# Group 1 of a convolution and MLP kernel: the run outermost on its partitions, one transfer each for x, y and output, and two first products moved ahead of a copy of w1

## The chip, the cores and the metric

The kernel runs on one core of a Trainium2 chip. The time is device time in microseconds of one execution. The engines are TensorE (PE, its weight loads PEld), VectorE (DVE), ScalarE (ACT), GpSimd (POOL) and SyncE (SP, which only issues DMAs here). DMAs are issued from SP's, ACT's or POOL's queue and are carried out by the core's 16 DMA engines.

## The reference

x has shape (8, 4224, 192), float32. First a causal depthwise convolution along the sequence with 7 taps; the taps are shared by the 24 channels of each of 8 heads and are a softmax over the 7. Then a residual block: normalise, multiply by a gain, up to 768 channels, ReLU, down to 192, add.

```python
w = exp(weight - max(weight)); w = w / (sum(w) + 1e-9)        # (8 heads, 7 taps)
y[b, s, h, :] = sum_k w[h, k] * x_pad[b, s + k, h, :]         # 6 zero rows ahead of x
yn = (y - mean(y)) / sqrt(var(y) + 1e-6) * g_ln
out = y + relu(yn @ w_ch1) @ w_ch2                            # 192 -> 768 -> 192
```

## The kernel before

**Groups.** The rows of x are cut into 17 groups (`groups`). A partition holds a run of neighbouring rows, with the 6 rows ahead of it, which the taps need. Of each batch the first 4096 rows lie as 128 runs of 32 rows; the 128 rows left of each of the 8 batches make up one group of their own, group 1 (`b is None`): 8 batches x 16 runs x 8 rows, one run to a partition. In the kernel before, partition 16 b + p holds run p of batch b, so each batch is a block of 16 neighbouring partitions, and each transfer of the group is made batch by batch: `load_x` (L141 to L148) issues batches 0 to 3 from SP and 4 to 7 from POOL, `store_y` (L487) issues eight stores from SP, `add_to_out` (L949) eight accumulating stores from POOL; the last two take their pieces from `rows_of_out`. All arithmetic is by partition and doesn't ask which row lies where.

**Stages of a group.** `first_tap` writes y = tap 0 times x on ACT (L378, one instruction for each head); `conv` adds the other taps on VectorE (L415); in some groups `second_tap` makes a product on ACT that a DMA adds. `transpose` turns y into 32 x 32 blocks on VectorE (L426). `up` multiplies by w1 on TensorE (L531) and `evict_up` writes the ReLU of it out of PSUM on ACT (L521). `down` multiplies by w2 (L796). The result, times the inverse deviation, is added to y, which has already been stored to the output, by an accumulating DMA (`add_to_out`). From group 2 on the products are made from quarters with fewer multiplications (L859).

**The order.** The kernel writes its order out by hand; each engine's instructions run in the order in which they are recorded, and semaphores hold one that needs another's result. A queue's DMAs are issued in order too.

**The start, where most of the change lies.** The weights come as 64-bit words and are put together by VectorE and ACT (`split_words`, `join_...`). `centre_w1` then makes the centred w1: three heads of group 0's convolution run on TensorE (`conv_on_pe`, L326, evicted at L330), and `copies_of_w1` copies rows of w1 to all four blocks of 32 partitions by matmuls (L352, L355), which ACT evicts into `w1` (L360): first chunks 0 to 3 of the left half, then chunks 4 and 5 of both halves, then `up(0)` begins. In `up(0)`, set f of 6 uses four PSUM banks, taken in turn from eight (`take_set`), and its matmuls go through the six chunks of w1 in order:

```python
banks = take_set()
rows_of_tiles(banks, yt[g][:, 0:n], w1[:, :, f * P : f * P + P])
evict_up(g, f, banks[:, :, 0 : n * C])
if g == 0 and f == 0:
    first_tap(1, heads=(0, H // 2))
elif g == 0 and f == 1:
    copies_of_w1(1, [(q, 1) for q in range(NQ)])
    scale_power(words_2[2])
elif g == 0 and f < 4:
    first_tap(1, heads=(2 * f, 2 * f + 2))
```

So ACT meets group 1's first four products between the evictions of set 0 and set 1. `copies_of_w1(1)` takes the four banks of set 0, so set 2 takes those of set 1 and waits for that eviction. `load_x(1)` is issued after the load of w2 (`raw`, L988), behind a small write of VectorE that holds it back (`gate`, L139).

Of the kernel before, what the change touches and what calls it, by code (L numbers as in the profile page):

```python
# [11 lines left out]
ALU = mybir.AluOpType  # L12
# [4 lines left out]
def kernel(  # L17
# [29 lines left out]
    nc = tc.nc  # L47
    PSUM = bass.MemoryType.PSUM
    B, S, D = x.shape
    H, K = weight.shape  # L50
    F = moe_w_ch1.shape[1]
    P = 128
# [3 lines left out]
    PAD = K - 1  # L56
    J = 16
    R = 2 * J
    LEFT = (S - P * R) * B // P
    LP = P // B  # L60
# [33 lines left out]
    def rows_of_out(g, j1, j2):  # L94

        b, j0, n = groups[g]
        if b is not None:
            return [(slice(0, P), outr[b, :, (j0 + j1) * D : (j0 + j2) * D])]
        left = out[:, P * R : S].rearrange("b (p r) d -> b p (r d)", p=LP)
        return [  # L100
            (slice(LP * b, LP * b + LP), left[b, :, j1 * D : j2 * D]) for b in range(B)
        ]

    consts = ctx.enter_context(tc.tile_pool(name="consts", bufs=1))
    xpool = ctx.enter_context(tc.tile_pool(name="xin", bufs=2))
# [14 lines left out]
    def take_bank():  # L120
        i = turn[0] % 8
        turn[0] = i + 1
        return all_banks[:, i]

    def take_set():
        i = (turn[0] + 3) // 4 * 4 % 8
        turn[0] = i + 4
        return all_banks[:, i : i + 4]
# [4 lines left out]
    def load_x(g, queue=nc.sync, pad=True, gate=False):  # L133
        b, j0, n = groups[g]
        t = xpool.tile([P, J + PAD, D], F32, tag="xg", name=f"xg{g}")
        xg[g] = t
        flat = t.rearrange("p j d -> p (j d)")
        if gate:
            nc.vector.memset(t[0 : 1 if b is not None else P, 0:1, 0:1], 0.0)  # L139
        if b is None:  # L140
            for b in range(B):  # L141
                (queue if b < B // 2 else nc.gpsimd).dma_start(  # L142
                    out=flat[LP * b : LP * b + LP, 0 : (PAD + n) * D],
                    in_=bass.AP(
                        tensor=x.tensor, offset=(b * S + P * R - PAD) * D,
                        ap=[[n * D, LP], [1, (PAD + n) * D]],
                    ),
                )  # L148
            return
        if j0:  # L150
            queue.dma_start(
                out=flat[:, 0 : (n + PAD) * D], in_=xr[b, :, (j0 - PAD) * D : (j0 + n) * D]
            )
            return
        if b:

            queue.dma_start(
                out=flat[:, 0 : (PAD + n) * D],
                in_=bass.AP(
                    tensor=x.tensor, offset=(b * S - PAD) * D, ap=[[R * D, P], [1, (PAD + n) * D]]  # L160
                ),
            )
            if pad:
                nc.gpsimd.memset(t[0:1, 0:PAD, :], 0.0)
            return
        nc.gpsimd.memset(t[0:1, 0:PAD, :], 0.0)
        for p0, p1 in ((16, P), (1, 16)):
            nc.sync.dma_start(
                out=flat[p0:p1, 0 : (PAD + n) * D],
                in_=bass.AP(  # L170
                    tensor=x.tensor, offset=(b * S + p0 * R - PAD) * D,
                    ap=[[R * D, p1 - p0], [1, (PAD + n) * D]],
                ),
            )
        nc.sync.dma_start(out=flat[0:1, PAD * D : (PAD + n) * D], in_=xr[b, 0:1, 0 : n * D])
# [38 lines left out]
    for s in range(2):  # L214
        nc.sync.dma_start(  # L215
            out=raw1[:, s].rearrange("p f w -> p (f w)"),
            in_=w1_words[0:P, 2 * FH * s : 2 * FH * (s + 1)],
        )
    for r in range(2):
        nc.sync.dma_start(  # L220
            out=raw1[Q * r : Q * r + Q, 2, :, :].rearrange("p f w -> p (f w)"),
            in_=w1_words[P:D, 2 * FH * r : 2 * FH * (r + 1)],
# [22 lines left out]
    def scale_power(power):  # L245
        nc.scalar.activation(power, power, AF.Relu, scale=float(1 << 23), bias=low)
# [52 lines left out]
    for q in range(NQ):  # L299
        m = copy[C * q : C * q + C].rearrange("p (q i) -> p q i", q=NQ)  # L300
        nc.gpsimd.affine_select(
            out=m, in_=m, pattern=[[0, NQ], [-1, C]],
# [9 lines left out]
        out=unit, in_=unit, pattern=[[-1, P]], compare_op=ALU.not_equal, fill=1.0, base=0,  # L312
# [4 lines left out]
    def tap_matrices(h, ks=range(K)):  # L317
        for k in ks:
            nc.scalar.mul(diag[:, h - PE_HEADS[0], k, :], unit, taps[:, h, k : k + 1])

    def conv_on_pe(h):
        n = groups[0][2]
        cs = slice(h * GRP, h * GRP + GRP)
        pc = take_bank()[:, 0 : n * GRP]
        for k in range(K):
            nc.tensor.matmul(  # L326
                pc, diag[:, h - PE_HEADS[0], k, :], xg[0][:, k : k + n, cs],
                start=(k == 0), stop=(k == K - 1),
            )
        nc.scalar.copy(y[0][:, 0:n, cs], pc.rearrange("p (j d) -> p j d", d=GRP))  # L330

    def centre_w1():
        pm = [take_bank()[:, 0:FH] for r in range(2)]
        for r in range(2):
            nc.tensor.matmul(pm[r], share[0], w1f[:, r, :], start=True, stop=False)
        conv_on_pe(PE_HEADS[2])
        for r in range(2):
            nc.tensor.matmul(pm[r], share[1 + r], w1f[:, 2, :], start=False, stop=True)
        tap_matrices(PE_HEADS[1], range(3))
        for r in range(2):  # L340
            nc.scalar.copy(mean[:, FH * r : FH * r + FH], pm[r])
        tap_matrices(PE_HEADS[1], range(3, K))
        conv_on_pe(PE_HEADS[0])
        copies_of_w1(0, [(q, 0) for q in range(NQ)])
        conv_on_pe(PE_HEADS[1])
        copies_of_w1(2, [(NQ, 0), (NQ + 1, 0), (NQ, 1), (NQ + 1, 1)])

    def copies_of_w1(s, parts):
        pw = [take_bank() for q in range(NQ)]
        for q in range(NQ):  # L350
            rows = slice(C * q, C * q + C)
            nc.tensor.matmul(pw[q][:, 0:FH], copy[rows], w1f[rows, s, :], start=True, stop=False)  # L352
        for q, (c, r) in enumerate(parts):
            rows = slice(C * q, C * q + C)
            nc.tensor.matmul(  # L355
                pw[q][:, 0:FH], less[rows], mean[rows, FH * r : FH * r + FH],
                start=False, stop=True,
            )
        for q, (c, r) in enumerate(parts):
            nc.scalar.copy(w1[:, c, FH * r : FH * r + FH], pw[q][:, 0:FH])  # L360
# [8 lines left out]
    def first_tap(g, heads=(0, H)):  # L369
        n = groups[g][2]  # L370
        if g == 1:

            y[g] = y[0][:, groups[0][2] :]
        elif heads[0] == 0:
            y[g] = ypool.tile([P, J, D], F32, tag="y", name=f"y{g}")
        for h in range(*heads):
            cs = slice(h * GRP, h * GRP + GRP)
            nc.scalar.mul(y[g][:, 0:n, cs], xg[g][:, 0:n, cs], taps[:, h, 0:1])  # L378
# [112 lines left out]
    def hidden_tile(g):  # L491
        n = groups[g][2]

        if fast[g]:
            ht[g] = room.rearrange(
                "p (h e f q j t) -> p h e f q j t", h=2, e=2, f=FC, q=NQ, t=width(g)
            )
        else:
            ht[g] = room[:, 0 : NF * NQ * n * C].rearrange(
                "p (f j q t) -> p f j q t", f=NF, q=NQ, t=C  # L500
            )
# [57 lines left out]
    def up(g):  # L559


        n = groups[g][2]
        hidden_tile(g)
        for f in range(NF):
            banks = take_set()
            rows_of_tiles(banks, yt[g][:, 0:n], w1[:, :, f * P : f * P + P])
            evict_up(g, f, banks[:, :, 0 : n * C])
            if g == 0 and f == 0:
                first_tap(1, heads=(0, H // 2))
            elif g == 0 and f == 1:  # L570
                copies_of_w1(1, [(q, 1) for q in range(NQ)])
                scale_power(words_2[2])
            elif g == 0 and f < 4:
                first_tap(1, heads=(2 * f, 2 * f + 2))
            between(g, f)
# [364 lines left out]
    def add_to_out(g, j1, j2):  # L940
        if groups[g][0] is None:

            j1, j2 = (0, j2) if j2 == groups[g][2] else (0, 0)
        for ps, rows in rows_of_out(g, j1, j2) if j2 else ():
            src = ots[g][ps, j1:j2].rearrange("p j d -> p (j d)")
            step = 4 * D if groups[g][0] is not None else (j2 - j1) * D
            for d0 in range(0, (j2 - j1) * D, step):
                d1 = min(d0 + step, (j2 - j1) * D)
                nc.gpsimd.dma_start(out=rows[:, d0:d1], in_=src[:, d0:d1], accum_op=ALU.add)  # L949

    def add(g, j, src):

# [28 lines left out]
    for s in range(3):  # L981
# [7 lines left out]
        out=raw2.rearrange("p (c d) w -> p c (d w)", d=D),  # L989
        in_=w2_words.rearrange("(c p) d -> p c d", p=P),  # L990
# [25 lines left out]
    for g in range(NG):  # L1016
# [3 lines left out]
        if mixed:  # L1020
            work = up_mixed(g, ahead(g), pending)
            pending = iter(())
        else:
            up(g)
            work = []
# [47 lines left out]
        if last:  # L1073
# [4 lines left out]
            for j in range(fast[g], groups[g][2]):  # L1078
                rows = take_bank()[:, 0:D]
# [36 lines left out]
```

## Time and profile before

| | |
|---|---|
| median of 3 runs | 950.75 us (949.05 to 951.53) |
| profiled execution, its own time | 948.58 us |
| its span, first to last instruction | 946.8 us |
| PE busy | 940.1 us (99%) |
| PEld, DVE, ACT, POOL busy | 745.7, 894.0, 699.4, 341.9 us |
| granted TensorE clock | 1.00 |
| group 1: loads of x, each 168 KB | 4 on SP, 4 on POOL |
| group 1: stores of y and of the output, each 96 KB | 8 on SP, 8 on POOL |

All times in the profile count from the span's start. An engine's busy time says nothing of what it waits for; the lists of waits say who ended an idle time, and the chain of waits follows the last instruction back to what released it. A row of the timeline gives start, duration, engine, line, operation, output<-inputs, shape and count, and in brackets the idle time ahead of it and who ended it.

### The profile page before, as it was taken

How to read it: one execution, taken by the hardware profiler on the slowest of the kernel's cores; microseconds unless marked ns; L12 is line 12 of the kernel's file. 1: busy time of each engine (PE TensorE's matmuls, PEld its weight loads, DVE VectorE, ACT ScalarE, POOL GpSimd, SP SyncE). 2: the span in 40 equal slices, each digit the busy share in tenths (PEclk: the TensorE clock that was granted, in tenths of full speed). 3: DMA queues.
4: the chain of work that ended last, by engine and by line, in shares of the span. 5: the costliest groups of instructions: out<-in, count | busy, mean ns of one | idle time of the engine just before them, and what ended most of it. 6: DMA issues, size and time to landing. Idle time of an engine off the chain costs nothing.

```text
span 946.8 us, 38072 instructions
## 1 busy us (share of the span) xinstructions
PE 940.1 (99%) x16900; PEld 745.7 (79%) x16900; DVE 894.0 (94%) x1498; ACT 699.4 (74%) x1250; POOL 341.9 (36%) x478
## 2 busy tenths in 40 slices
PE   9999999999999999999999999999999999999998
PEld 7998896877869687786968778696877869696787
DVE  8999999999999999999999999999999999999867
ACT  6763688596878969687896968779696877967362
POOL 2157522723145141533227141452316332261420
PEclk9999999999999999999999999999999999999999
DMA  8359699689797988979697897969889797778261
GB/s 207 111 152 212 107 239 272 125 189 232 135 270 134 252 162 184 223 134 279 127 254 150 204 217 130 280 132 250 162 194 214 131 275 136 174 136 136 52 114 68
DMA packets 39833, 169.35 MB, mean 179 GB/s; under 512 B 4469, under 2 KB 8182, under 8 KB 33655
## 3 DMA queue, kind: packets, MB, share of 16 engines
q0 software_dynamic: 32992, 107.46, 61.3%
q1 hardware_dynamic: 6672, 59.47, 16.9%
q8 instruction: 132, 2.16, 0.9%
q14 instruction: 31, 0.25, 0.1%
q10 hardware_dynamic: 6, 0.00, 0.0%
HBM read 38.93 MB, written 50.33 MB: 94 GB/s over the span
## 4 chain that ended last, share of the span: by engine, by line
PE 97%; DMA 2%; DVE 0%; ACT 0%; POOL 0%; SPq 0%; issue 0%; ACTq 0%; DVEq 0%
PE ps L531 48%; PE ps L859 44%; PE ps L796 4%; DMA xg<-in_x_dram 1%; DMA room<-in_moe_w_ch_dram 1%; DVE room L266 0%; POOL xg L142 0%; ACT y L378 0%; DVE room L256 0%; SPq L215 0%; ACT room L521 0%; SPq L220 0%; DVE room L250 0%; DVE y L953 0%; DVE room L239 0%
## 5 line engine op out<-in xcount | busy, mean ns | idle before, releaser
L415 DVE SCALAR_TENSOR_TENSOR y<-xg,taps,y 128x384 f32<-128x384 f32 (+3 forms) x720 | 364.3, 580 | 3.0 <-DMA y<-room 1.9
L859 PE MATMUL ps<-room,w2sums 128*32 128x256 f32 (+2 forms) x4608 | 244.9, 371 | 0.0
L531 PE MATMUL ps<-yt,w 32*128 32x256 f32 (+2 forms) x4160 | 237.8, 373 | 0.5 <-ACT room L521 0.5
L531 PEld LDWEIGHTS ps<-yt,w 32*128 32x128 f32 x4160 | 210.8, 185 | 21.9 <-issue 6.5
L859 PEld LDWEIGHTS ps<-room,w2sums 128*32 128x32 f32 x4608 | 149.7, 110 | 89.3
L660 ACT COPY room<-ps 128x512 f32<-128x512 f32 (+1 forms) x213 | 174.1, 858 | 62.0 <-PE ps L531 62.0
L859 PE MATMUL ps<-room,w 128*32 128x256 f32 (+2 forms) x3456 | 188.6, 371 | 0.0
L826 DVE TENSOR_TENSOR room<-room 128x1024 f32<-128x1024 f32 (+2 forms) x147 | 161.2, 1169 | 21.4 <-PE ps L859 14.8
L859 PEld LDWEIGHTS ps<-room,w 128*32 128x32 f32 x3456 | 110.7, 110 | 70.1 <-DVE room L666 5.0
L531 PE MATMUL ps<-ysums,w1sums 32*128 32x256 f32 x2160 | 126.6, 375 | 0.0
L531 PEld LDWEIGHTS ps<-ysums,w1sums 32*128 32x128 f32 x2160 | 116.3, 185 | 4.8
L949 POOL DMA_DIRECT2D out_dram<-ot x69 | 58.9, 950 | 162.6 <-ACT ot L938 159.1
L865 ACT COPY cs<-ps 128x256 f32<-128x256 f32 (+2 forms) x192 | 70.2, 368 | 45.0 <-PE ps L859 44.9
L407 POOL DMA_DIRECT2D y<-tb x59 | 52.1, 1373 | 138.6 <-ACT room L865 104.6
L673 ACT ACTIVATE room<-room 128x1024 f32<-128x1024 f32 (+1 forms) x89 | 94.4, 1073 | 3.5 <-DMA room<-parts_cs 3.4
L938 ACT ACTIVATE ot<-ot,r 128x192 f32<-128x192 f32 x224 | 94.7, 468 | 0.0
L378 ACT ACTIVATE y<-xg,taps 128x384 f32<-128x384 f32 (+3 forms) x141 | 73.1, 607 | 1.0 <-DMA xg<-in_x_dram 0.7
L446 DVE BATCH_NORM_STATS2 st<-y 128x6 f32<-128x192 f32 x264 | 70.2, 343 | 0.0
L531 PE MATMUL ps<-yt,w1sums 32*128 32x256 f32 x1080 | 69.2, 376 | 0.0
L865 ACT COPY room<-ps 128x256 f32<-128x256 f32 (+2 forms) x96 | 35.4, 370 | 44.5 <-PE ps L859 43.6
L531 PE MATMUL ps<-ysums,w 32*128 32x256 f32 x1080 | 68.3, 374 | 0.0
L396 ACT ACTIVATE tb<-xg,taps 128x384 f32<-128x384 f32 (+1 forms) x120 | 66.1, 630 | 0.0
(120 smaller groups left out, 937.7 us busy)
## 6 DMA issues: line engine op xcount, KB each, us to landing
xg<-in_x_dram SPq DMA_DIRECT2D x14, 2112.0 KB, 16.4
room<-room POOLq DMA_DIRECT2D x45, 512.0 KB, 5.1
out_dram<-ot POOLq DMA_DIRECT2D x59, 384.0 KB, 9.3
y<-tb POOLq DMA_DIRECT2D x58, 384.0 KB, 8.4
out_dram<-y SPq DMA_DIRECT2D x13, 1536.0 KB, 9.8
room<-parts_cs POOLq DMA_DIRECT2D x28, 512.0 KB, 7.1
room<-parts_tb POOLq DMA_DIRECT2D x14, 1024.0 KB, 7.6
xg<-in_x_dram POOLq DMA_DIRECT2D x1, 2112.0 KB, 15.4
```

What stands on the lines that cost most here:

```text
L378: nc.scalar.mul(y[g][:, 0:n, cs], xg[g][:, 0:n, cs], taps[:, h, 0:1])
L396: nc.scalar.mul(tb[g][:, 0:n, cs], xg[g][:, 1 : 1 + n, cs], taps[:, h, 1:2])
L415: nc.vector.scalar_tensor_tensor(out=y[g][:, 0:n, cs], in0=t[:, k : k + n, cs], scalar=taps[:, h, k : k + 1], in1=y[g][:, 0:n, cs], op0=AL ...
L446: nc.vector.bn_stats(out=sums[g][:, j, :], in_=y[g][:, j, :])
L531: nc.tensor.matmul(banks[:, q, i * w + j1 * t : i * w + j2 * t], right[rows, c, P * i : P * i + P], left[rows, j1:j2, c, :], start=start, ...
L660: nc.scalar.activation(to, of, AF.Relu) if relu else nc.scalar.copy(to, of)
L673: nc.scalar.activation(c, c, AF.Relu)
L826: nc.vector.tensor_tensor(a[:, *dst, f], a[:, *left, f], a[:, *right, f], op=op)
L859: nc.tensor.matmul(dst[C * q : C * q + C, 0:w], right[:, f, C * c : C * c + C], left[:, f, q], start=(first and f == PAIR), stop=(f == PAI ...
L865: nc.scalar.copy(to[:, c], dst[:, 0:w].rearrange("p (j t) -> p j t", t=t))
L938: nc.scalar.mul(ots[g][:, j, :], ots[g][:, j, :], rstd[g][:, j : j + 1])
L949: nc.gpsimd.dma_start(out=rows[:, d0:d1], in_=src[:, d0:d1], accum_op=ALU.add)
```

## The change

Partition 8 p + b now holds run p of batch b. As the runs are the outer index and the batches the inner one, all 128 partitions can be written in a single access pattern, and group 1's load of x (now on SP alone), its store of y and its accumulating store become one transfer each. And two of the four first products that stood between the evictions of set 0 and set 1 move ahead of the copies of w1's chunks 4 and 5: on ACT they now stand between L330 (the last head convolved on TensorE) and L360. The number of matmuls, vector instructions and activations, and their sizes, stay as they are.

```diff
 def rows_of_out(g, j1, j2):
-        left = out[:, P * R : S].rearrange("b (p r) d -> b p (r d)", p=LP)
-        return [
-            (slice(LP * b, LP * b + LP), left[b, :, j1 * D : j2 * D]) for b in range(B)
-        ]
+        left = out[:, P * R : S].rearrange("b (p r) d -> p b (r d)", p=LP)
+        return [(slice(0, P), left[:, :, j1 * D : j2 * D])]
...
 def load_x(g, queue=nc.sync, pad=True, gate=False):
...
         if b is None:
-            for b in range(B):
-                (queue if b < B // 2 else nc.gpsimd).dma_start(
-                    out=flat[LP * b : LP * b + LP, 0 : (PAD + n) * D],
-                    in_=bass.AP(
-                        tensor=x.tensor, offset=(b * S + P * R - PAD) * D,
-                        ap=[[n * D, LP], [1, (PAD + n) * D]],
-                    ),
-                )
+            queue.dma_start(
+                out=flat[:, 0 : (PAD + n) * D],
+                in_=bass.AP(
+                    tensor=x.tensor, offset=(P * R - PAD) * D,
+                    ap=[[n * D, LP], [S * D, B], [1, (PAD + n) * D]],
+                ),
+            )
             return
...
 def centre_w1():
...
         conv_on_pe(PE_HEADS[1])
+        first_tap(1, heads=(0, H // 4))
         copies_of_w1(2, [(NQ, 0), (NQ + 1, 0), (NQ, 1), (NQ + 1, 1)])
...
 def up(g):
...
             if g == 0 and f == 0:
-                first_tap(1, heads=(0, H // 2))
+                first_tap(1, heads=(H // 4, H // 2))
...
 def add_to_out(g, j1, j2):
...
-                nc.gpsimd.dma_start(out=rows[:, d0:d1], in_=src[:, d0:d1], accum_op=ALU.add)
+                nc.gpsimd.dma_start(out=rows[..., d0:d1], in_=src[:, d0:d1], accum_op=ALU.add)
```

## The prediction

> **What bounds the kernel now.** I read the page first: TensorE (PE) is busy for 940.1 of 946.8 us. So I asked for TensorE's waits:
>
> ```profile
> PE ps L211 <- DMA room<-in_weight_dram: 2.1, 1, 2.1
> PE ps L531 <- ACT room L521: 0.5, 1, 0.5
> ```
>
> Each line tells who waited for whom, the total, the count and the longest. There are two waits in the whole run. With the 4.1 us after its last matmul (942.68 to 946.8) they make up the 6.7 us in which TensorE is not busy. The first wait (taps' weights, before 3 us) and the tail lie outside the change, so only the second, 0.50 us, can be won. The chain of waits says where it is (start, duration, what):
>
> ```profile
> 12.87 1.66 POOL xg L142 x3
> 14.52 11.56 DMA xg<-in_x_dram
> 26.08 0.12 issue
> ...
> 26.36 1.49 ACT y L378 x4
> 27.85 0.70 ACT room L521
> 28.55 0.04 issue
> 28.60 8.08 PE ps L531 x192
> 36.68 11.90 PE ps L796 x72
> ```
>
> The last of the eight loads of group 1's x lands at 26.08; then ACT makes four first products (L378), then evicts group 0's second set of banks (L521), then TensorE goes on. After 28.60 the chain is TensorE to its end: a microsecond won or lost before 28.60 moves the whole run by as much, if nothing off TensorE falls behind. The timelines of ACT and TensorE around it:
>
> ```profile
> 21.21 0.28 ACT L330 COPY y<-ps 128x144 f32<-128x144 f32 x1 [0.31 <-PE ps L326]
> 22.70 1.63 ACT L360 COPY w<-ps 128x384 f32<-128x384 f32 x4 [1.20 <-PE ps L355]
> 24.18 1.20 ACT L234 ACTIVATE spare<-spare 128x1152 f32<-128x1152 int32 x1
> 25.25 0.83 ACT L521 ACTIVATE room<-ps 128x768 f32<-128x768 f32 x1
> 26.36 1.49 ACT L378 ACTIVATE y<-xg,taps 128x192 f32<-128x192 f32 x4 [0.28 <-issue]
> 27.76 0.78 ACT L521 ACTIVATE room<-ps 128x768 f32<-128x768 f32 x1
> ```
>
> ```profile
> 22.50 4.09 PE L531 MATMUL ps<-yt,w 32*128 32x192 f32 x96
> 26.53 0.93 PE L352 MATMUL ps<-room 32*128 32x384 f32 x8
> 27.17 0.93 PE L355 MATMUL ps<-room 32*128 32x384 f32 x8
> 28.60 8.08 PE L531 MATMUL ps<-yt,w 32*128 32x192 f32 x192 [0.50 <-ACT room L521]
> ```
>
> ACT is idle for 1.2 us before L360 (21.49 to 22.70) and is the late one at 27.76: TensorE finished the second set at 26.59 and the next eight matmuls at 28.10, while ACT gave the banks back at 28.54.
>
> **The moved products.** Four products take 1.49 us, so two take about 0.75. Taken out of the place at 26.36, they let the next eviction follow earlier: the first eviction ends at 26.08, the wait for x (0.28) is gone if x is there, two products run from about 26.0 to 26.7, and the eviction, whose matmuls ended at 26.59, runs from 26.7 to 27.5. TensorE needs it at 28.10, so 0.6 us is left over and the wait of 0.50 goes. What is late next is TensorE itself.
>
> In the new place the two stand ahead of L360 on ACT's queue. If x has landed by 21.5, they fill 21.5 to 22.25 of the idle 1.2 us: cost nothing, hidden by the wait for L355. If that cover is gone, everything behind them on ACT waits: L360, L234 (for which VectorE waits at L250) and both evictions. TensorE needs L360's first copy when it comes to the fifth of six chunks of w1: each set's matmuls take 2.05 us, so at 22.50 + 4 x 0.34 = 23.87. A copy takes 0.49 us, so L360 may start at 23.35; less 0.71 for the products and 0.28 from landing to start, x may land at 22.3. From there each microsecond costs one.
>
> **When x lands.** The change makes eight loads of 16 partitions (four on SP's queue, four on POOL's) one load of 128 on SP's, behind the load of w2. No row shows a load whose DRAM side has 16 runs by 8 batches, so I bound it by rows. Three stretches of the trace (us, busy by engine, clock, DMA share, GB/s):
>
> ```profile
> 7.00:10.00 3.00, 3.00 (x14) 2.98 (x15) 2.81 (x8) 2.70 (x9) 0.00 (x0) 1.00 0.99 283
> 16.50:23.50 7.00, 7.00 (x84) 5.39 (x86) 7.00 (x23) 4.40 (x14) 0.00 (x0) 1.00 0.99 159
> 25.00:28.50 3.50, 3.10 (x56) 2.35 (x48) 3.03 (x7) 3.22 (x8) 0.00 (x0) 1.00 1.04 436
> ```
>
> The middle one is these eight loads: the DMA engines are full, at only 159 GB/s. The last is group 0's store and group 2's load, 128 partitions each: as full, at 436. The first is group 0's load of 112 partitions: 283. The new load moves 128 x 10752 B = 1.376 MB. By the windows of a microsecond each, w2's 1.18 MB have passed at about 15.8. At 436 the load takes 3.2 us, at 283 4.9, at 159 8.7. From last byte to landing I add 0.6 (the load of group 2: last packets end near 30.5, landed 31.08) and, for the slow end, 1.5. So x lands at 19.6, 21.5 or 26.0. I take the first two as likely, because the load spans all 128 partitions like theirs; both come before 22.3, so both give the same sum.
>
> [...]
>
> **The rest, at nothing.** SP issues one load for four (1.72 us at 12.58; its next issue is at 21.63) and POOL none for four (2.16 us at 12.87; its next work is at 44.02). The store of group 1's y, eight issues on SP from 51.55 to 60.43, becomes one; SP's next issue is at 116.44, and ACT, which writes that buffer again, comes at 65.82, after the old landing of 62.97. A store that landed later than 65.8 would cost ACT time, but that ACT work serves matmuls that begin at 116.93. The eight accumulating stores on POOL (92.92 to 98.95) become one; POOL's next work waits for VectorE until 100.74 anyway. So some 1, 8 and 5 us of SP and POOL are freed, and nobody waits for them.
>
> **What must follow.** TensorE 0.5 us earlier needs its inputs earlier. Tightest is VectorE's second transpose of group 1, done at 47.46, wanted at 48.51 by the next up projection, whose later chunks it feeds: 1.05 us of room, 0.55 afterwards. w2 is ready at 34.92 for use at 36.6. Later transposes have over 10 us.
>
> **Sum.** -0.50 (the wait) + 0 (products in the gap) + 0 (queues) = -0.5 us: span 946.3. The profiled execution took 948.58, 1.77 more than its span, so 948.1. That execution lies 2.2 below the median of the runs (950.75); from the median, 950.2. A kernel of this time cannot be told from no change within about 0.3% (2.85 us): the three runs span 2.5. So the forecast is no measurable difference, with a true gain of 0.05%.
>
> **Rivals.**
> 1. The gain is lost again: something with the 0.55 us of room, or VectorE at 94% busy, falls behind, and the span stays. For it: VectorE is nearly full. Against: VectorE waits for TensorE, not TensorE for it (no such line among TensorE's waits). Time 950.75.
> 2. Slower: x lands too late, and ACT stands at the products with L360 behind them. This begins at a landing after 22.3 and costs more than the 0.5 won after about 22.8. At the slow end, 26.0: products 26.3 to 27.0, L360's first copy done at 27.5 instead of by 23.87 (+3.6); the first eviction ends at 30.4, the second at 31.9, TensorE goes on at 31.95 instead of 28.60: +3.3, thus 954.1, just over 0.3%. For it: the bytes are the same, all sit in one queue behind w2, and the shape is new. Against: the rows of 283 and 436. [...]
> 3. The change doesn't do what it says: the mixed shape runs on fewer DMA engines. Half of them at 436/2 GB/s: 6.3 us, landing 22.7, no net change; a quarter: 12.6 us, landing 29.0, about +6, 957. No row shows such a transfer.
>
> **How the numbers follow.** Forecast 0.72, rival 1 0.13, rival 2 0.07, rival 3 0.05 (half of it slower), 0.03 for what I don't see. A gain over 0.3% has no place in the profile, since TensorE idles 0.5 us there: only scatter gives it, 0.04. Slower: rival 2, half of rival 3, and scatter, 0.10. The same: 0.86. The runs reach from 1.7 below to 0.8 above their median; with the same scatter both ways around 950.2 and 950.75 the range is 948.4 to 952.4, and what is left out is rival 2, the slow half of rival 3, and some scatter.
>
> **What would show it.** Right: x's load in one issue, landed before 22.3, in a stretch well above 159 GB/s; two first products between 21.5 and 22.3; L360 still at 22.70; the second eviction at about 26.7; only the wait of 2.1 us left to TensorE; a span near 946.3. Wrong: a wait of ACT on x before L360, a wait of TensorE on L360 near 23.9, or a new wait of TensorE near 48.

## The result: 0.1 to 0.2% slower, and x lands too late for its new place

Twelve runs each: the changed kernel 951.66 us (949.57 to 954.39), the kernel before 949.69 (948.58 to 951.53). The ratio is 1.0021, with a 95% interval of 1.0012 to 1.0030: slower by about 2 us, where the forecast was no measurable difference with a true gain of 0.5 us. The time lies within the forecast's range (948.4 to 952.4), but above the kernel before and not below it. Two later measurements, on two chips, gave 1.0010 (0.9998 to 1.0022) and 1.0008 (0.9999 to 1.0017). Each of them just includes no change; the three together speak for a loss of 1 to 2 us, rather nearer to 1. The profiled execution took 950.69 us, its span 948.9.

TensorE's waits in the changed kernel (who waited for whom, total us, count, longest):

```profile
PE ps L208 <- DMA room<-in_weight_dram: 2.1, 1, 2.1
PE ps L529 <- ACT w L358: 0.8, 1, 0.8
PE ps L323 <- DMA xg<-in_x_dram: 0.7, 1, 0.7
PE ps L332 <- DVE raw L985: 0.6, 1, 0.6
PE ps L857 <- issue: 0.2, 1, 0.2
```

The wait on the eviction (L521, now L519) is gone, as forecast. In its place stands one on L358, the copies of w1 into SBUF: what rival 2 named. (The lines on L323 and L332 are no loss: both are ahead of the landing of group 0's x, which sets the pace there; in this execution the warm-up matmuls ran faster, 25 in the 3.0 us from 6.5 against 24 in the 5.0 us from 6.5 before, and left TensorE idle ahead of it.) ACT's timeline of the stretch:

```profile
20.89 0.28 ACT L327 COPY y<-ps 128x144 f32<-128x144 f32 x1 [0.31 <-PE ps L323]
23.47 0.80 ACT L376 ACTIVATE y<-xg,taps 128x192 f32<-128x192 f32 x2 [2.29 <-DVE spare L230]
24.18 1.59 ACT L358 COPY w<-ps 128x384 f32<-128x384 f32 x4
25.64 1.19 ACT L231 ACTIVATE spare<-spare 128x1152 f32<-128x1152 int32 x1
26.71 0.82 ACT L519 ACTIVATE room<-ps 128x768 f32<-128x768 f32 x1
27.40 0.82 ACT L376 ACTIVATE y<-xg,taps 128x192 f32<-128x192 f32 x2
28.09 0.83 ACT L519 ACTIVATE room<-ps 128x768 f32<-128x768 f32 x1
```

ACT stands from 21.17 to 23.47 at the two moved products, because x lands at 23.39 and not by 21.5. The page puts the 2.29 us down to VectorE, but that is its guess at which of two semaphores came last: VectorE's part in this wait is the small write that holds the load back, done at 12.4. In another profile of the same kernel the idle time at this place bears the right name:

```profile
24.13 0.80 ACT L376 ACTIVATE y<-xg,taps 128x192 f32<-128x192 f32 x2 [2.45 <-DMA xg<-in_x_dram]
```

Then TensorE, in the changed kernel's profile:

```profile
22.27 1.58 PE L529 MATMUL ps<-yt,w 32*128 32x192 f32 x32
24.68 3.19 PE L529 MATMUL ps<-yt,w 32*128 32x192 f32 x63 [0.83 <-ACT w L358]
...
28.34 0.99 PE L353 MATMUL ps<-room 32*128 32x384 f32 x8
28.98 1.32 PE L529 MATMUL ps<-yt,w 32*128 32x192 f32 x24
```

It does four chunks of w1 (32 matmuls), waits 0.83 us for the fifth, and begins the third set at 28.98 instead of 28.60, now without a wait. That is 0.4 us. The spans of the two profiles differ by 2.1 us, and the rest does not come from this place: some 2.0 us are small gaps of TensorE after 100 us, which the further profiles below take up, and the tail behind its last matmul is 0.4 us shorter. And the load itself, in the stretch in which it alone is moving (us, busy by engine, clock, DMA share, GB/s):

```profile
16.00:21.50 5.50, 5.50 (x50) 4.24 (x53) 5.50 (x21) 3.96 (x12) 0.00 (x0) 1.00 0.98 213
```

The DMA engines are as full as with the eight loads (0.98 for 0.99), which ran at 159 GB/s, and half as quick as in the stretch with the store of group 0 and the load of group 2, 128 partitions each (436).

### The profile page after: what moved, and what is told of

Same layout as the page of the kernel before. It is cut to its first block, busy times and chain, and to the rows that moved or that the text cites. A ratio compares the mean times of both kernels' runs of the same rounds, so it can differ in the third digit from the quotient of the medians.

```text
span 948.9 us, 38028 instructions
## 1 busy us (share of the span) xinstructions
PE 940.7 (99%) x16900; PEld 749.4 (79%) x16900; DVE 893.8 (94%) x1498; ACT 699.8 (74%) x1250; POOL 335.2 (35%) x467
## 4 chain that ended last, share of the span: by engine, by line
PE 97%; DVE 1%; DMA 1%; SPq 0%; ACT 0%; issue 0%; DVEq 0%
PE ps L529 49%; PE ps L857 44%; PE ps L794 4%; DMA xg<-in_x_dram 1%; DVE y L413 1%; SPq L217 0%; ACT y L376 0%; PE ps L350 0%; SPq L212 0%; DVE yt L424 0%; DVE spare L230 0%; PE ps L353 0%; SPq L165 0%; DVE y L951 0%; ACT w L358 0%
## 5 line engine op out<-in xcount | busy, mean ns | idle before, releaser
L857 PEld LDWEIGHTS ps<-room,w2sums 128*32 128x32 f32 x4608 | 152.4, 110 | 87.6 <-issue 0.7
L857 PEld LDWEIGHTS ps<-room,w 128*32 128x32 f32 x3456 | 112.7, 110 | 69.1 <-DVE room L664 5.0
L947 POOL DMA_DIRECT2D out_dram<-ot x62 | 53.4, 879 | 162.1 <-ACT ot L936 161.0
```

What stands on the lines that cost most here:

```text
L857: nc.tensor.matmul(dst[C * q : C * q + C, 0:w], right[:, f, C * c : C * c + C], left[:, f, q], start=(first and f == PAIR), stop=(f == PAI ...
L947: nc.gpsimd.dma_start(out=rows[..., d0:d1], in_=src[:, d0:d1], accum_op=ALU.add)
```

## The experiments

The theories: **A**, the loss is x's landing behind the two products, with w1's copies queued behind them on ACT; **B**, it sits in the single transfers themselves, above all the stores; **C**, it is chance.

**The products back in their old place, the layout kept.**

```diff
         conv_on_pe(PE_HEADS[1])
-        first_tap(1, heads=(0, H // 4))
...
-                first_tap(1, heads=(H // 4, H // 2))
+                first_tap(1, heads=(0, H // 2))
```

> The changed kernel with all four products back between the evictions of set 0 and set 1 (the layout and the single transfers stay). Theory A (the loss is ACT standing at the two moved products until x lands at about 23.4 us, with the copies of w1 behind them): the wait is gone, x at 23.4 is before the old place at 26.0, so L358 starts at about 22.5 and TensorE loses at most 0.3 us there; span 946.5 to 947, time 0 to 0.4 us under the kernel before. Theory B (the loss sits in the single transfers themselves, above all the stores, later in the run): about 2 us slower than before, as the changed kernel. Theory C (chance gaps in TensorE's issue, any kernel can have them): median within 1 us of before, with single runs 2 to 4 us higher.

Measured: 948.16 us against 949.21, ratio 0.9988 (0.9979 to 0.9998): 1.05 us faster than before, more than the 0 to 0.4 us expected. x lands at 23.29, as in the changed kernel, but its first reader comes only after the first eviction, at 24.72. TensorE's sets 0 and 1 run through, and the third follows at once:

```profile
21.38 4.18 PE L528 MATMUL ps<-yt,w 32*128 32x192 f32 x96
...
26.00 0.85 PE L352 MATMUL ps<-room 32*128 32x384 f32 x8
26.99 4.33 PE L528 MATMUL ps<-yt,w 32*128 32x192 f32 x98
```

Theory B falls: all three single transfers are in this kernel, and it is faster than the kernel before. The gain was already in the joined load; the move of the products spent it.

**The products moved, the old loads kept.**

```diff
         conv_on_pe(PE_HEADS[1])
+        first_tap(1, heads=(0, H // 4))
...
-                first_tap(1, heads=(0, H // 2))
+                first_tap(1, heads=(H // 4, H // 2))
```

> The kernel before with only the two products moved ahead of the copies of w1; x still comes in eight loads of 16 partitions, last landed near 26 us. Theory A: ACT stands until 26.1 to 26.4, the first copy of w1 is done at 27.5 instead of 23.2, TensorE waits about 3.5 us and goes on with its third set near 31.9: 3.0 to 3.5 us slower than before (span near 950). Theory B: as before, within 0.5 us. Theory C: no steady difference.

Measured: 954.42 us against 949.21, ratio 1.0052 (1.0034 to 1.0069), runs from 951.18 to 957.02. The last of the eight loads landed at 27.91 in the profile, and ACT and TensorE waited for it:

```profile
28.21 0.80 ACT L379 ACTIVATE y<-xg,taps 128x192 f32<-128x192 f32 x2 [6.41 <-DMA xg<-in_x_dram]
```

```profile
22.80 1.48 PE L532 MATMUL ps<-yt,w 32*128 32x192 f32 x32
29.42 4.38 PE L532 MATMUL ps<-yt,w 32*128 32x192 f32 x64 [5.14 <-ACT w L361]
```

The direction is A's, and with an interval that stays over 3 us theory C falls for this kernel. The size is larger than expected, for two reasons. The landing was 1.9 us later than the 26.0 that the sum was made for. And TensorE's granted clock fell behind so long a wait (the last three figures of the row are clock, DMA share and GB/s):

```profile
29.40:33.80 4.40, 4.38 (x68) 4.38 (x72) 2.19 (x4) 3.56 (x7) 0.00 (x0) 0.65 0.15 61
```

so that 64 matmuls took 4.38 us, which take 2.73 at the usual rate (96 in 4.09). The clock stood at half from 29.11, 4.8 us after TensorE had run out of work, to 32.52. The third set came at 34.92, 6.3 us later than in the kernel before. In the mean of the stretch behind the 5.1 us of waiting the clock was 0.65; behind the changed kernel's 0.83 us it was 1.00 (24.7 to 27.7). The runs of this kernel are spread over 5.8 us, those of the kernel with the products in their old place over 2.4. Theory A would have it so, since with the products ahead of w1's copies the landing's scatter goes into the time; the landings of the runs that were not profiled are not known.

**x ahead of w2.**

```diff
         if s == 1:
+            load_x(1, gate=True)
             nc.vector.memset(raw2[0:1, 0:1, :], 0)
...
-    load_x(1, gate=True)
```

> The changed kernel with group 1's load of x issued ahead of the load of w2 (same gate place, order of the two swapped). Theory A: x starts near 11.2 us, takes about 6 us and lands near 18.5, long before 21.2; w2 lands near 21.5, just before VectorE reads it at 22.7; the two products fill ACT's gap, no wait of TensorE on ACT is left, third set at about 28.1: 0.4 to 0.6 us faster than before, 2.4 faster than the changed kernel. Theory B: 2 us slower than before. Theory C: scatter alone.

Measured: 949.76 us against 949.21, ratio 1.0007 (0.9998 to 1.0015). A miss by about 1 us. x did land early (19.91), and the products fit the gap; but w2 landed at 24.52, not 21.5, and the wait moved to VectorE's first step on w2, on which ACT's L231 depends, with the evictions behind that:

```profile
22.76 1.63 ACT L358 COPY w<-ps 128x384 f32<-128x384 f32 x4 [0.51 <-PE ps L353]
25.33 1.17 ACT L231 ACTIVATE spare<-spare 128x1152 f32<-128x1152 int32 x1 [0.94 <-DVE spare L230]
26.40 0.79 ACT L519 ACTIVATE room<-ps 128x768 f32<-128x768 f32 x1
```

Two loads share one stretch of DMA time, and ACT's queue waits for both, for w2 by way of VectorE; swapping them swaps who waits: x landed at 19.91 instead of 23.39, w2 at 24.52 instead of 17.05 in the changed kernel's profile. In the place that counts it stands level with the kernel before: from the start of the convolution's last eviction on ACT (L327, before L330) to TensorE's third set 7.36 us pass, 7.39 in the kernel before and 8.09 in the changed one.

**The load with 128 rows on both sides.**

```diff
-                    ap=[[n * D, LP], [S * D, B], [1, (PAD + n) * D]],
+                    ap=[[n * D, P], [1, (PAD + n) * D]],
```

> The changed kernel, but the load of group 1's x reads 128 neighbouring runs in DRAM, so that both sides of the transfer have 128 rows (group 1 then computes on other rows of x; bytes, partitions and the rest are the same). If the mixed shape (16 x 8 rows in DRAM on 128 partitions) is what makes the load slow: packets of 10752 B take about 0.41 us instead of 0.79, the load runs near 430 GB/s, lands near 20 us, no wait of ACT on x, 0.4 to 0.6 us faster than before. If the load is slow for another reason (its place behind w2, HBM): packets near 0.8 us, landing near 23.4, time as the changed kernel.

This kernel leaves out the right rows of group 1, so its output is not the reference's; the work is the same. Measured: 948.09 us against 949.21, ratio 0.9988 (0.9979 to 0.9997), 1.1 us faster than before where 0.4 to 0.6 was expected. The load runs at 394 GB/s and lands at 19.98:

```profile
16.00:19.00 3.00, 3.00 (x31) 2.36 (x29) 3.00 (x12) 2.17 (x8) 0.00 (x0) 1.00 0.94 394
```

The rest then goes as the prediction had it, with the products in the gap and the evictions early:

```profile
21.30 0.28 ACT L327 COPY y<-ps 128x144 f32<-128x144 f32 x1 [0.30 <-PE ps L323]
21.48 0.80 ACT L376 ACTIVATE y<-xg,taps 128x192 f32<-128x192 f32 x2
22.79 1.63 ACT L358 COPY w<-ps 128x384 f32<-128x384 f32 x4 [0.51 <-PE ps L353]
...
26.74 0.82 ACT L519 ACTIVATE room<-ps 128x768 f32<-128x768 f32 x1
```

As many bytes to the same partitions from the same place in the queue: only the DRAM side differs, in shape and in addresses. The products in the gap show in the profile, where the third set begins 6.48 us after the start of the convolution's last eviction, against 7.00 with the products in their old place; in the medians (948.09 and 948.16) this difference is not to be seen.

**The same, with the rows far apart in DRAM.**

```diff
-                    tensor=x.tensor, offset=(P * R - PAD) * D,
-                    ap=[[n * D, LP], [S * D, B], [1, (PAD + n) * D]],
+                    tensor=x.tensor, offset=0,
+                    ap=[[B * S * D // P, P], [1, (PAD + n) * D]],
```

> As the kernel with 128 neighbouring runs in DRAM, but the 128 runs lie 202,752 B apart, spread over all of x (group 1 again computes on other rows). It parts two readings of that experiment: if the DRAM side's shape (128 rows, not 16 x 8) is what made the load fast, it stays at 0.40 us a packet and near 390 GB/s and lands near 20 us, with no wait of TensorE on ACT. If neighbouring addresses in DRAM made it fast, it falls back to about 0.77 us a packet and 213 GB/s and lands near 23.4.

This kernel too computes group 1 on other rows. One run: 947.94 us, span 946.2, and in the same stretch

```profile
16.00:19.00 3.00, 3.00 (x29) 2.07 (x28) 3.00 (x13) 2.10 (x8) 0.00 (x0) 1.00 1.05 432
```

So with 128 rows on the DRAM side the load is no slower with the rows far apart (432 GB/s) than with neighbours (394). What is left is the shape of 16 x 8, or the step of 3,244,032 B between the batches that comes with it; no run parts these two. The landing was 21.57 here and not near 20: the last packet of the load ended only 0.3 us later than with neighbouring rows (19.70 for 19.42), but the semaphore's full count came 1.9 us behind it, for 0.6 there, the last two of its sixteen steps at 20.96 and 21.57. Why is not known. ACT waited 0.61 us for it, TensorE not at all.

**One load, the batch outermost.**

```diff
-            for b in range(B):
-                (queue if b < B // 2 else nc.gpsimd).dma_start(
...
+            queue.dma_start(
+                out=flat[:, 0 : (PAD + n) * D],
+                in_=bass.AP(
+                    tensor=x.tensor, offset=(P * R - PAD) * D,
+                    ap=[[S * D, B], [n * D, LP], [1, (PAD + n) * D]],
+                ),
+            )
```

> The kernel before (its layout, its eight stores, its products in their old place) with the eight loads of x joined into one: DRAM side 8 batches x 16 runs. If the load is shared out by the outermost index, 8 DMA engines take 16 neighbouring partitions each: packets of 10752 B, 16 to an engine, 6.5 us at 0.41 us each or 12.7 us at 0.79, and the DMA share in the stretch is near 0.5 instead of 1.0. Landing near 23.5 or near 30; in the second case ACT waits some 4 us for x and the run is 3 to 4 us slower than before. If all 16 engines share it: share near 1.0, landing between 20 and 24, time at or below the kernel before.

The old order of the partitions, too, lets one transfer write all of them; the new order was not needed for that. One run: 959.89 us. While the load is alone, about half of the DMA engines' time is used (0.53):

```profile
17.00:20.00 3.00, 3.00 (x29) 2.08 (x28) 3.00 (x12) 2.10 (x8) 0.00 (x0) 1.00 0.53 118
```

```profile
31.63 1.49 ACT L377 ACTIVATE y<-xg,taps 128x192 f32<-128x192 f32 x4 [6.01 <-DMA xg<-in_x_dram]
```

That is rival 3's case: with 8 as the outermost index the share is near that of 8 engines of 16. The load's semaphore fits it: eight steps of its count come late, from 28.73 to 31.61, where the changed kernel's load has sixteen, from 22.27 to 23.39. x was there at 31.6, 1.6 us later than the slow branch of the expectation, and the loss is about 10 us instead of 3 to 4: ACT waited 6.0 us, TensorE 6.3 and began its third set at 33.87 instead of 28.60, and then its clock was at half, which the expectation had left out:

```profile
33.90:38.00 4.10, 4.10 (x52) 4.10 (x56) 4.10 (x13) 2.57 (x5) 0.00 (x0) 0.50 0.06 27
38.00:41.00 3.00, 3.00 (x56) 3.00 (x52) 2.97 (x5) 1.50 (x3) 0.00 (x0) 0.68 0.00 0
```

Here the clock fell at 29.71, 2.1 us after TensorE's last matmul (27.60), and stayed at half until 39.95, 6.1 us into the work.

**w2 one step earlier.**

```diff
-        if s == 1:
+        if s == 0:
             nc.vector.memset(raw2[0:1, 0:1, :], 0)
```

> The changed kernel with the gate of w2's load one step earlier (after the first third of w1 is joined, about 9.3 us, instead of the second, 10.9). The DMA engines stand nearly idle from 10.5 to 12.3 us before; now w2 fills that stretch and passes by about 14.3, so group 1's x starts 1.5 us earlier and lands near 22.0 to 22.5. Theory A: the two products end at about 23.0, TensorE loses nothing or up to 0.2 us at the copies of w1: 0.3 to 0.9 us faster than before, 1.5 to 2.5 faster than the changed kernel. If the loss were not in the landing: as the changed kernel, 1 to 2 us slower than before.

Measured: 949.20 us against 950.00, ratio 0.9991 (0.9981 to 1.0000). x lands at 22.84, the products start at 22.92 and TensorE has no wait on ACT any more:

```profile
22.92 0.80 ACT L376 ACTIVATE y<-xg,taps 128x192 f32<-128x192 f32 x2 [0.80 <-DMA xg<-in_x_dram]
```

Its third set begins 6.64 us after the start of the convolution's last eviction, against 8.09 in the changed kernel. It is 0.8 us faster than before at the median, the interval just reaching no change, and 1.0 us faster than the changed kernel on the same chip (950.20), where 1.5 to 2.5 had been expected.

**Further profiles of the changed kernel and the one before.**

> The changed kernel as it is. Its twelve runs fell into two bunches (949.6 to 950.7 and 952.6 to 954.4); the kernel before and the one with the products back show one. Theory A says that the upper bunch has x landing later: a profile with a long time has the load's landing at 25 to 27 us instead of 23.4, ACT's wait at the moved products 4 to 6 us, TensorE's wait on L358 2.5 to 4 us; a profile with a short time has the landing at 22.5 to 23.5 and a wait of TensorE under 1 us. Theory C says that the difference lies after 30 us, in gaps of TensorE's issue, with the landing always near 23.4. Median 1.5 to 2.5 us above before.

> The changed kernel, one more look. Theory A: time = about 949.3 + (landing of x - 22.3) us, within 1 us of scatter. Theory C: no such relation; the landing stays near 23.4 and the difference comes after 30 us.

> The changed kernel, a third look. Theory A: time = about 949.3 + (landing of x - 22.3) us, within 1 us of scatter. Theory C: no such relation.

> The changed kernel on another chip again, for the size of the loss: Theory A says 0.4 to 2.0 us over the kernel before on the same chip, landing of x between 23 and 25 us in the profile, and single runs 3 us higher where it lands later. Theory C (chance): within 0.3 us of the kernel before.

> The kernel before, a second look. If the small gaps of TensorE after 100 us that the profiles of the changed kernel and of the variants show (0.3 to 2 us in sum) are chance, this profile has some as well, though the first one of this kernel had none. If they come from the change, it has none.

Measured: the changed kernel 950.54 us against 949.36 (the ratio 1.0010 above), 951.16 and 950.05 in single runs, and 950.20 against 950.00 (1.0008). x landed at 24.05, 23.76, 23.85 and 22.98, and TensorE waited 1.0, 1.2, 0.8 and 0.5 us for the copies of w1. By the landing alone the order is not right. Counted from the start of the convolution's last eviction, which moves from one execution to the next, x landed 2.64, 2.90, 2.29 and 1.92 us later, and 2.50 in the first profile: from 1.9 to 2.9 us the wait grows from 0.5 to 1.2, as A has it. The five times lie within 1 us of A's formula, but also within 0.7 us of 950.5, so they don't test it. The upper bunch, the other thing A spoke of, was not met again: one of 25 later runs was above 952 (953.99), and it was not profiled. The loss of 1.2 us was below the 1.5 to 2.5 expected.

The kernel before took 950.42 in its second profile. There its own last load landed at 27.11 (26.1 in the first profile), and ACT stood for it ahead of the second eviction, and TensorE behind that:

```profile
25.49 0.83 ACT L521 ACTIVATE room<-ps 128x768 f32<-128x768 f32 x1
27.34 1.49 ACT L378 ACTIVATE y<-xg,taps 128x192 f32<-128x192 f32 x4 [1.02 <-issue]
...
29.58 1.74 PE L531 MATMUL ps<-yt,w 32*128 32x192 f32 x35 [0.63 <-ACT room L521]
```

So the kernel before pays for late landings too, in the old place. Its sets began at 22.74, and with the 5.60 us from there to 28.10 that the first profile shows, TensorE could have gone on at 28.34: 1.2 us are lost there, where the prediction's profile had 0.50. That the joined load alone won 1.05 us fits with this. The profile also shows a small gap of TensorE far behind the change:

```profile
855.37 2.87 PE L531 MATMUL ps<-yt,w1sums 32*128 32x256 f32 x48 [0.28 <-ACT room L660]
```

Such gaps after 100 us come to between 0.8 and 2.1 us in every profile but two: none in the first of the kernel before, about 3 with the batch outermost. (Sum of the delays of TensorE against that first profile.) They are in kernels with and without the change, and they are as large as the loss that is to be explained.

## Why the prediction was wrong

**What bounds the kernel, and where**: right in the place. It was the wait at the third set; it went, and what came after followed TensorE. That 0.50 us is all there is to win was one execution's figure; the second profile of the kernel before loses 1.2 us there.

**The threshold and its price**: right, and closely. The prediction let x land until 22.3 and the copies of w1 start until 23.35. They started at 24.18, 0.83 us too late, and TensorE waited 0.83. Against the 0.50 won at the third set that is +0.33; the profile has +0.38 (28.98 for 28.60). That the two agree so well is partly luck, since TensorE came to its first set 0.23 us sooner in this execution (22.27 for 22.50), and by the landing itself, 1.09 us past 22.3, the price would have been 0.59: from landing to start 0.08 us passed, for the 0.28 of the sum. With x at 27.91 the sum gives 27.9 - 22.3 - 0.5 = 5.1 us at the third set; there it was 6.3. The slower clock adds 1.65 us to the sum (4.38 for 2.73), which is 0.4 too much; the steps around it were shorter.

**When x lands**: the step that failed. Of the three rows the prediction took the two faster ones, 436 and 283 GB/s, as nearest, "because the load spans all 128 partitions like theirs", and counted on 19.6 or 21.5. The load ran at 213, between the middle row and the slow one: its last packet ended at 22.37 and it landed 1.0 us later, at 23.39; in five profiles at 22.98 to 24.05, always past the threshold. (The middle landing of the sum, 15.8 + 4.9 + 0.6, is 21.3 and not 21.5, which changes nothing; for the 1.5 us of the slow end no row was given; from the last packet's end to the landing the runs showed 0.6 to 1.9 us.) Partitions were the wrong likeness. With 128 rows on both sides the load runs at 394 and 432 GB/s, with 16 x 8 rows on the DRAM side and the same 128 partitions at 213. The range of landings, 19.6 to 26.0, had held the answer; rival 2 got 0.07 where the bounds themselves gave no ground for so little.

**Rival 2**: right in its mechanism, though priced only at its far end. Between 22.8 and 26.0 its cost runs from nothing to 3.3 us, and the measured case lies in that stretch. What it left out is TensorE's clock, which was 0.65 and 0.50 in the mean of the 4 us behind waits of 5.1 and 6.3 us. That the bytes are the same, which it had for it, did not keep x's landing where it was: at equally full engines (0.98 and 0.99) the joined load ran at 213 GB/s for 159, and landed 2.7 us sooner than the last of the eight in the first profile before.

**Rival 3**: not this kernel (share 0.98), but the batch-outermost load is near it (0.53). Its price for half the rate, 218 GB/s and 6.3 us, is nearly what the changed kernel's load ran at, with the engines full: as a figure for this kernel that is luck.

**The rest, at nothing**: nothing speaks against it. POOL's wait for VectorE in place of the eight stores is 9.55 us long, and the two kernels with all single transfers and no late x are 1.1 us faster than before. The sign of rival 1, a new wait of TensorE near 48, is absent, though the room shrank: the second transpose was done at 48.68, for an up projection that began at 48.95.

**What stays open.** From the start of the convolution's last eviction to the third set 7.5 to 8.5 us pass in five profiles of the changed kernel (8.05 in the mean), 7.4 and 8.1 in two of the one before: the profiles explain 0.3 us of loss in the mean, 0.7 between the two first profiles. The medians gave 2.0, 1.2 and 0.2 us. So the experiments show what the loss comes from (it goes when x lands in time or the products go back, and grows with the later landing of the old loads), and the profiles don't show its size. Six of the first twelve runs were above 952.6, and none of those was profiled. A landing some microseconds later, with the clock's fall behind the wait, would do it: two of the six have a mean clock of 0.998, as most long runs of the kernel with the old loads and moved products have (0.996 to 0.998), but another, the longest, has 1.000. So this is argued, not shown. Whether the small late gaps are a little longer with the change (1.6 us in the mean of five profiles; 0 and 0.8 in two of before; 0.8 to 1.9 in five kernels with single transfers and no wait of TensorE for x) can't be told from so few.

## What to carry to other kernels

Work moved into an idle gap of an in-order queue carries its own wait with it (here ACT stood 2.29 us, and the copies of w1 behind it started at 24.18 for 22.70): find out when its input lands before asking how long the gap is, for what stands behind it on that queue waits too, and the landing's scatter (22.98 to 24.05 in five profiles) becomes the kernel's. The layout alone was worth 0.12% (0.02 to 0.21), and the move gave it back. The rate of a joined transfer could not be told here from its partitions or its bytes (the same at 213 and at 394 GB/s); the row to look for has the same outer sizes on both sides, and if there is none, keep both ends with their full chances.

## What the runs showed of the hardware

- As many bytes (1.376 MB) into the same 128 partitions, from the same queue, at engines 0.94 to 1.05 full: 394 and 432 GB/s with 128 rows on both sides, 213 with 16 x 8 rows in DRAM. By packets of 10752 B that is some 0.41 (with neighbouring rows: 110 packets above 8 KB in the 3 us from 16 to 19, at a share of 0.93 of 16 engines) against 0.77 us (107 packets in the 5 us from 16 to 21, at a share of 1.03).
- With 8 x 16 rows in DRAM the DMA engines were busy for 0.53 of their time, at 118 GB/s, and eight steps of the semaphore's count came late (28.73 to 31.61); with the changed kernel's 16 x 8 rows it was 0.98, 213 GB/s and sixteen steps (22.27 to 23.39). That 8 engines worked there and 16 here is an estimate from these shares and steps.
- Why the load with 16 x 8 rows is only half as quick as those with 128, at equally full engines, was not shown. The step between the batches in DRAM remains as a candidate (the eight loads, none of which has that step within it, were slow too, at 159 GB/s); which engine wrote which partition no run here shows.
- Behind waits of 5.1 and 6.3 us TensorE's granted clock was 0.65 and 0.50 in the mean of the next 4 us; behind 0.83 us it stayed at 1.00. It fell 4.8 and 2.1 us into those waits and came back 3.1 and 6.1 us after them.
- From the end of the last packet to the semaphore's full count 0.6 to 1.1 us passed in the five profiles of the changed kernel, 0.6 and 1.9 us in the two with 128 rows on both sides: the landing scatters by more than the shapes differ in this.
